# A statically ordered attention and MLP kernel: the order made anew with the sync queue's own issue times, large fetches in pieces, loads in order of use, memsets later

## Chip, cores, metric

One core of one Trainium2 chip. Time is device microseconds of a whole execution. The kernel before takes 810.61 us (median of 3 runs, 808.94 to 811.46). The profile's span, from first to last instruction, is about 2 us shorter than the time of the same execution (807.7 against 809.51); all stage times below are within the span. A profile is one execution.

## The reference, cut to what matters

```python
x: (1, 2048, 640); wqkv: (640, 1920); H = 32 heads of 20; F = 1536
g = sigmoid((x * gate_w).sum(-1))
a = softmax_attention(x, wqkv, wo)                 # scores, softmax, values, output projection
h = x @ w1 + b1;  b = (h * tanh(softplus(h))) @ w2 # mish
out = g * a + (1 - g) * b
```

## The kernel before

A list scheduler in Python (`Order`) runs when the program is built. Every piece of work is a `Task` with an engine, a declared cost, dependencies, a priority and a place in the order (`after`). It keeps a clock for each engine and emits the pieces as their turn comes. What runs on the chip is the resulting fixed sequence on each engine, with semaphores between engines. A declared cost is therefore never executed; it only moves work about in the sequence.

The attention works on groups G of four heads by 512 queries. Of a group's 16 key tiles, `SHARE[G]` go through VectorE (an approximate exponential by integer arithmetic), the others through ScalarE's exponential, two instructions of 128 x 1024 each. The last group is cut in two halves.

```python
class Task:                      # (cut)
        self.need, self.issue = 1e9, 450      # ns for which the sync queue is believed taken by one issue
...
    ld_x = {0: [load_x(("AQ", "SP")[s % 2], s, s + 1, 4200) for s in range(4)]}   # AQ: ACT's DMA queue
    ld_w0 = [load(("SP", "AQ")[t], w0[:, t], ..., 4500) for t in range(2)]        # first queries', keys' weights
    ld_x[1] = [load_x("SP", 4, 8, 6500)]
    ld_wv = load("SP", wv, w_src[:, :, 2 * D:3 * D], 8000)                        # values' weights
    ld_x[2] = [load_x("AQ", 8, 12, 9000)]
...
    # each group's end: denominators gathered, inverted, spread to DRAM, broadcast, multiplied
    t1 = o.add("SP", 2200, gather, [t0], prio=0, key=G)
    t2 = o.add("DVE", 245, rec, [t1], prio=2, key=G)
    t3 = o.add("SP", 2200, spread, [t2], prio=0, key=G)      # "rows<-rec" in the profile: 8 KB, 4 KB for the half group at the end
    t4 = o.add("SP", 3000, bcast, [t3], prio=0, key=G, rings=[rb])   # "rbc<-rows", 4 DMAs
    t5 = o.add("DVE", 690, norm, [t4], ...)                  # "on<-oraw,rbc"
...
    # near the end: heads and MLP sums come back from DRAM, then the output projection
    def back(c):
        def fetch():
            if c < 3:
                nc.sync.dma_start(out=bs_of(c)..., in_=bsd[c])                       # 640 KB
            nc.sync.dma_start(out=ocs[c][:, 0:KT - 1, :], in_=ocd[c]...)             # 512 KB, "w<-oc"
            nc.sync.dma_start(out=ocs[c][0:48, KT - 1, :], in_=ocd[c][(KT - 1) * P:...])
```

The projection of the first two quarters of the output uses PSUM tile X, of which there is one; that of the last two uses the three S tiles. VectorE mixes the result with the MLP's ("xt<-X,g,w") and so frees the tile.

The softmax here doesn't subtract the row's maximum and nothing guards it: scores larger than these inputs give would overflow.

## Time and profile before

| stage (us of the span) | before |
|---|---|
| start to first exponential | 11.93 |
| first to 22nd exponential | 24.76 |
| 22nd to end of the last of 740 | 749.0 |
| tail, after the last exponential | 22.0 |
| ScalarE idle: up to the 22nd / from there to the last | 5.1 / 10.0 |

The 22nd exponential is a fair post for the end of the start, at about 36 us, when loads end. ScalarE and TensorE are each about 95% busy, so look at the two ends and at gaps. The prediction shows the lines.

### The profile page before, as it was taken

To read this page: it belongs to the slowest core of one execution; us is meant where nothing else is said; L and a number is where in the kernel's file an instruction comes from. 1 tells how busy PE (TensorE), PEld (TensorE's weight loads), DVE (VectorE), ACT (ScalarE), POOL (GpSimd) and SP (SyncE) were. 2 spreads that over 40 slices of the span, in tenths; PEclk is the share of its full clock that TensorE was granted. 3 is DMA by queue.
4 is the path that set the end of the run, shared out by engine and by line. 5 is a ranking of instruction groups with operands and counts; after the bars stand their busy time and mean duration, and the time that the engine had idled before them with its cause. 6 is when DMAs were issued, how large, how long until landed. Compare 5 with 4: busy or idle time off the path is not lost.

```text
span 807.7 us, 25538 instructions
## 1 busy us (share of the span) xinstructions
PE 768.4 (95%) x11228; PEld 279.7 (35%) x11228; DVE 683.4 (85%) x906; ACT 763.3 (95%) x791; POOL 9.7 (1%) x12
## 2 busy tenths in 40 slices
PE   7999999999899998999999999899999997999978
PEld 3433223222443334333323332433223222243445
DVE  3699799999977878999798789889999998978934
ACT  4899999999999999999999999999999999899990
POOL 4000000000000000000000000000000000000000
PEclk9999999999999999999999999999999999999999
DMA  9602100112001000011110112111100002212132
GB/s 309 199 23 57 27 23 23 36 46 65 21 29 46 23 24 25 20 54 35 48 30 22 26 35 68 30 37 38 28 10 20 19 19 81 72 28 72 37 87 84
DMA packets 45608, 39.88 MB, mean 49 GB/s; under 512 B 20244, under 2 KB 39380, under 8 KB 45496
## 3 DMA queue, kind: packets, MB, share of 16 engines
q1 hardware_dynamic: 44024, 37.14, 15.9%
q8 instruction: 88, 1.44, 0.8%
q10 hardware_dynamic: 1472, 1.10, 0.4%
q14 instruction: 24, 0.20, 0.1%
HBM read 26.63 MB, written 11.08 MB: 47 GB/s over the span
## 4 chain that ended last, share of the span: by engine, by line
PE 51%; ACT 33%; DVE 7%; DMA 5%; issue 3%; SPq 1%; DVEq 0%; ACTq 0%
ACT es L890 26%; PE S L865 20%; PE C L848 15%; PE X L584 10%; ACT arena L1071 6%; PE X L667 3%; DVE t L924 3%; PE S L584 2%; DMA rbc<-rows 1%; DMA rows<-rec 1%; DMA wvt<-in_A_wqkv_dram 1%; DVE t L938 1%; ACT L1070 1%; PE X L646 1%; SPq L1018 1%
## 5 line engine op out<-in xcount | busy, mean ns | idle before, releaser
L890 ACT ACTIVATE es<-S 128x1024 bf16<-128x1024 f32 x740 | 683.1, 1131 | 16.7 <-PE S L865 16.0
L924 DVE TENSOR_SCALAR t<-S 128x1024 uint16<-128x1024 f32 x284 | 345.5, 1219 | 34.9 <-PE S L865 33.6
L865 PE MATMUL S<-qs,kt 32*128 32x512 bf16 (+1 forms) x2112 | 313.0, 376 | 14.5 <-ACT es L890 6.7
L865 PEld LDWEIGHTS <-kt 32*128 32x128 bf16 x2112 | 94.4, 91 | 282.3 <-issue 271.1
L938 DVE TENSOR_SCALAR t<-t 128x2048 uint16<-128x2048 uint16 x284 | 186.7, 683 | 3.8 <-PE C L848 2.2
L848 PE MATMUL C<-es,va 128*32 128x512 bf16 (+1 forms) x1536 | 136.3, 379 | 0.5 <-DVE oraw L972 0.4
L848 PE MATMUL C<-t,vs 128*32 128x512 bf16 (+1 forms) x1152 | 103.1, 380 | 0.9 <-DVE t L938 0.6
L584 PE MATMUL X<-xt,w 128*32 128x512 bf16 x960 | 75.3, 383 | 1.2 <-DVE arena L1057 1.2
L584 PE MATMUL X<-w,arena 128*32 128x320 bf16 x1536 | 76.3, 305 | 0.1
L848 PEld LDWEIGHTS <-va 128*32 128x32 bf16 x2112 | 48.7, 95 | 73.7 <-issue 66.0
L1071 ACT ACTIVATE arena<-arena 128x2048 bf16<-128x2048 bf16 x36 | 69.1, 1939 | 0.3
L848 PE MATMUL C<-t,va 128*32 128x512 bf16 (+1 forms) x576 | 56.2, 379 | 2.8 <-DVE oraw L972 2.3
L584 PEld LDWEIGHTS <-arena 128*32 128x32 bf16 x1856 | 41.4, 96 | 41.3 <-issue 33.1
L667 PE MATMUL X<-xt,wqk 128*32 128x512 bf16 (+1 forms) x640 | 51.0, 383 | 0.0
L584 PEld LDWEIGHTS <-w 128*32 128x32 bf16 (+1 forms) x1280 | 29.0, 97 | 34.2 <-issue 27.1
L848 PEld LDWEIGHTS <-vs 128*32 128x32 bf16 x1152 | 29.5, 95 | 31.3 <-issue 25.9
L1057 DVE TENSOR_SCALAR arena<-X,b 128x512 bf16<-128x512 f32 x48 | 35.8, 745 | 4.7 <-PE X L584 4.6
L584 PE MATMUL X<-wvt,xt 128*32 128x160 bf16 x1240 | 28.2, 233 | 8.0 <-DVE va L724 4.8
L1025 DVE TENSOR_TENSOR on<-oraw,rbc 128x512 bf16<-128x512 f32 (+1 forms) x32 | 21.7, 678 | 13.8 <-DMA rbc<-rows 13.5
L584 PEld LDWEIGHTS <-xt 128*32 128x32 bf16 x1280 | 23.4, 96 | 18.1 <-issue 16.2
L673 DVE CAST g<-X 120x512 bf16<-120x512 f32 x32 | 21.9, 684 | 3.9 <-PE X L667 3.8
L972 DVE COPY oraw<-C 128x512 f32<-128x512 f32 (+1 forms) x33 | 22.0, 667 | 1.3 <-PE C L848 1.3
(80 smaller groups left out, 249.2 us busy)
## 6 DMA issues: line engine op xcount, KB each, us to landing
rbc<-rows SPq DMA_DIRECT2D x124, 64.0 KB
w<-in_B_w_dram SPq DMA_DIRECT2D x2, 1920.0 KB
out_dram<-xt SPq DMA_DIRECT2D x16, 160.0 KB
oc<-on SPq DMA_DIRECT2D x112, 20.0 KB
k<-g SPq DMA_DIRECT2D x16, 120.0 KB
kt<-k SPq DMA_DIRECT2D x24, 80.0 KB
q<-g SPq DMA_DIRECT2D x16, 120.0 KB
qs<-q SPq DMA_DIRECT2D x96, 20.0 KB
```

What stands on the lines that cost most here:

```text
L584: nc.tensor.matmul(t[32 * r:32 * r + 32, 0:width], lhsT=lhsT(r), rhs=rhs, start=a, stop=b, tile_position=(0, 32 * r))
L667: nc.tensor.matmul(t[32 * r:32 * r + w, 0:QC], lhsT=wqk[:, k, a:a + w], rhs=xt[:, c, k, :], start=k == 0, stop=k == KT - 1, tile_position= ...
L673: nc.vector.tensor_copy(out=gb.tile, in_=t[0:120, 0:QC])
L848: nc.tensor.matmul(acc[G][32 * r:32 * r + 32, qa:qb], lhsT=vs4[:, b, term - 1, DVE_KEYS.index(j), h:h + 32] if term else va4[:, b, j, h:h ...
L865: nc.tensor.matmul(t[:, (off + a) * QC + i * w:(off + a) * QC + (i + 1) * w], lhsT=kt[32 * r:32 * r + 32, (p % 2) * S + j * P:(p % 2) * S ...
L890: nc.scalar.activation(eb.tile[:, 0:w * QC], sb.tile[:, 0:w * QC], ACT.Exp, scale=inv)
L924: nc.vector.tensor_scalar(out=bufs[0].tile[:, 2 * QC * hp:2 * QC * (hp + 1)], in0=xb.tile, scalar1=P * LOG2E * inv, scalar2=P * (127 - log ...
L938: (nc.vector if eng == "DVE" else nc.gpsimd).tensor_scalar(out=bufs[i].tile[:, a * w:(a + 1) * w], in0=bufs[0].tile[:, a * w:(a + 1) * w], ...
L972: nc.vector.tensor_copy(out=ob.tile[:, a:b], in_=acc[G][:, a:b])
L1025: nc.vector.tensor_tensor(out=nb.tile[:, qa:qb], in0=ob.tile[:, qa:qb], in1=rb.tile[:, qa:qb], op=ALU.mult)
L1057: lambda t: nc.vector.tensor_scalar(out=hs[:, ft, :], in0=t[:, 0:QC], scalar1=b1[:, ft:ft + 1], scalar2=None, op0=ALU.add),
L1071: nc.scalar.activation(v, hs[:, 4 * a:4 * a + 4, :] if i == 0 else v, func, bias=1.0 if i == 1 else 0.0)
```

## The change

Intent: give the scheduler the sync queue's real issue times, so that its order fits the chip better; split fetches so that short transfers get between them; load x and then the values' weights on one queue in order of use; move memsets behind what is urgent; then choose the places of all work anew.

```diff
-SHARE = (2, 4, 4, 5, ... 5, 5, 2, 2)
+SHARE = (3, 6, 5, 2, ... 4, 3, 4, 4)
-DENSE = (0.8, 6.7, 11.35, 19.15)          # likewise MISH, DOWN, KEYS, QUERIES, VALUES
+DENSE = (1.25, 4.7, 11.7, 18.4)
-OUT = (26.25, 26.8, 28.9)
+OUT = (26.05, 27.7, 27.55)
-LEAD = 32
+LEAD = 24
-        self.need, self.issue = 1e9, 450
+        self.need, self.issue = 1e9, issue          # default 350
-    OVER = 900  LOW = 3  AHEAD = 8  EARLY = 600  BESIDE = 120
+    OVER = 1200 LOW = 2  AHEAD = 24 EARLY = 550  BESIDE = 30
-    nc.gpsimd.memset(kt[:, S:2 * S], 0.0)
-    nc.gpsimd.memset(qs, 0.0)
+    t_zero = [o.add("POOL", 1800, lambda a=a: nc.gpsimd.memset(a, 0.0), prio=3) for a in (kt[:, S:2 * S], qs)]
-    ld_x[1] = [load_x("SP", 4, 8, 6500)]
-    ld_wv = load("SP", wv, ..., 8000)
-    ld_x[2] = [load_x("AQ", 8, 12, 9000)]
-    ld_x[3] = [load_x("SP", 12, 16, 11000)]
+    ld_x[1] = [load_x("SP", 4, 8, 6000)]
+    ld_x[2] = [load_x("SP", 8, 12, 8000)]
+    ld_x[3] = [load_x("SP", 12, 16, 10000)]
+    ld_wv = load("SP", wv, ..., 12500)
-        for i in range(10):     # warm-up matmuls
+        for i in range(8):
-        t1 = o.add("SP", 2200, gather, ...)
+        t1 = o.add("SP", 2050, gather, ..., issue=560)
-        t3 = o.add("SP", 2200, spread, ...)
+        t3 = o.add("SP", 1600, spread, ..., issue=350)
-        t4 = o.add("SP", 3000, bcast, ...)
+        t4 = o.add("SP", 3600, bcast, ..., issue=1700)
-    def fetch(): (640 KB, 512 KB, 48 KB, one task)
+    t_back[c]: four tasks of 128 KB, one of 48 KB, four of 160 KB (issue=900 each)
... (issue times of other fetches, the late loads' place, cut)
```

More of the change, by code (lines that the diff above doesn't have):

```diff
@@ L34 @@
 DVE_KEYS = (1, 4, 7, 10, 13, 14)
-SHARE = (2, 4, 4, 5, 4, 5, 5, 6, 3, 3, 4, 5, 5, 6, 2, 5, 6, 3, 4, 6, 4, 4, 6, 6, 4, 5, 6, 6, 2, 5, 5, 2, 2)
-DENSE = (0.8, 6.7, 11.35, 19.15)
-MISH = (0.9, 3.35, 2.65, 4.9)
-DOWN = (-0.75, -1.85, 4.0, 8.2)
-KEYS = ((0, 0.95, 2.2), (1, 5.5, 5.65), (2, 11.55, 13.85), (3, 18.55, 19.15), (4, 24.1, 24.45))
-QUERIES = 1.6
-VALUES = ((1, 2.8), (2, 10.0), (3, 12.4))
-OUT = (26.25, 26.8, 28.9)
+SHARE = (3, 6, 5, 2, 5, 4, 4, 6, 3, 5, 5, 5, 5, 5, 4, 4, 6, 4, 3, 6, 5, 4, 5, 4, 5, 4, 6, 4, 5, 4, 3, 4, 4)
+DENSE = (1.25, 4.7, 11.7, 18.4)
+MISH = (2.4, 4.2, 0.25, 3.7)
+DOWN = (-0.85, -1.2, 4.15, 7.5)
+KEYS = ((0, 0.8, 1.45), (1, 5.2, 7.45), (2, 13.05, 14.0), (3, 17.65, 18.85), (4, 24.55, 25.05))
+QUERIES = 2.05
+VALUES = ((1, 3.1), (2, 10.6), (3, 12.7))
+OUT = (26.05, 27.7, 27.55)
 PAIRS = 8
@@ L97, in __init__ @@
     def __init__(self, eng, cost, fn, deps=(), after=None, prio=5, rings=(),
-                 frees=(), mode=None, rows=(), key=0, port=False, work=0):
+                 frees=(), mode=None, rows=(), key=0, port=False, work=0, issue=350):
         self.eng, self.cost, self.fn = eng, cost - (84 if eng == "DVE" else 0), fn
@@ L134 @@
     LAT = {"PE": 230, "ACT": 165, "DVE": 134}
-    OVER = 900
-    LOW = 3
-    AHEAD = 8
+    OVER = 1200
+    LOW = 2
+    AHEAD = 24
     LATE = 28
     HOLD = 650
-    EARLY = 600
-    BESIDE = 120
+    EARLY = 550
+    BESIDE = 30
     AHEAD_D = 2000
@@ L497 @@
     ld_w0 = [load(("SP", "AQ")[t], w0[:, t], w_src[:, :, D * t:D * t + 92], 4500) for t in range(2)]
-    ld_x[1] = [load_x("SP", 4, 8, 6500)]
-    ld_wv = load("SP", wv, w_src[:, :, 2 * D:3 * D], 8000)
-    ld_x[2] = [load_x("AQ", 8, 12, 9000)]
-    ld_x[3] = [load_x("SP", 12, 16, 11000)]
-    ld_wqk = load("SP", wqk[:, :, 0:2 * D], w_src[:, :, 0:2 * D], 14000)
-    ld_gw = load("SP", gw[:, :, 0:1], gate_w.rearrange("(kt p o) -> p kt o", p=P, o=1), 8000)
+    ld_x[1] = [load_x("SP", 4, 8, 6000)]
+    ld_x[2] = [load_x("SP", 8, 12, 8000)]
+    ld_x[3] = [load_x("SP", 12, 16, 10000)]
+    ld_wv = load("SP", wv, w_src[:, :, 2 * D:3 * D], 12500)
+    ld_wqk = load("SP", wqk[:, :, 0:2 * D], w_src[:, :, 0:2 * D], 17500)
+    ld_gw = load("SP", gw[:, :, 0:1], gate_w.rearrange("(kt p o) -> p kt o", p=P, o=1), 18500)
+    ld_wqk.issue, ld_gw.issue = 2600, 2400
     t_ident = o.add("POOL", 1500, lambda: make_identity(nc, ident), prio=0)
@@ L513 @@
     t_pad = o.add("POOL", 700, lambda: nc.gpsimd.memset(wov[:, 5, :], 0.0), prio=2)
-    t_va = o.add("POOL", 6000, lambda: nc.gpsimd.memset(va, 1.0), prio=1)
+    t_va = o.add("POOL", 5000, lambda: nc.gpsimd.memset(va, 1.0), prio=1)
+    t_zero = [o.add("POOL", 1800, lambda a=a: nc.gpsimd.memset(a, 0.0), prio=3) for a in (kt[:, S:2 * S], qs)]
     junk = Buf(R["X"])
@@ L520, in warm @@
         junk.tile = pt(junk)
-        for i in range(10):
+        for i in range(8):
             nc.tensor.matmul(junk.tile[:, :], lhsT=kt[:, 0:P], rhs=kt[:, 0:QC], start=True, stop=True)
-    t_warm = o.add("PE", 4300, warm, [], prio=1.05, mode="full", rings=[junk], frees=[junk])
+    t_warm = o.add("PE", 3900, warm, [], prio=1.05, mode="full", rings=[junk], frees=[junk])
     t_warm.key = -1
@@ L693, in fetch @@
                                   in_=kd[u][DH * i:DH * i + DH, :])
-        t = o.add("SP", 4600, fetch, [t_kd[u, c] for u in {u for _, u, _ in pieces(p)} for c in range(NQ)],
+        t = o.add("SP", 4600, fetch, t_zero + [t_kd[u, c] for u in {u for _, u, _ in pieces(p)} for c in range(NQ)],
                   prio=1, key=g_of(p, 0) - 1, rings=[k_buf[p]])
-        t.issue = 1800
+        t.issue = 1300
         for j in range(NS):
@@ L707, in fetch @@
                                   in_=qd[u][DH * i:DH * i + DH, c * QC:(c + 1) * QC])
-        t_q[G] = o.add("SP", 4000, fetch, [t_qd[u, c] for u in {u for _, u, _ in pieces(p)}],
+        t_q[G] = o.add("SP", 4000, fetch, t_zero + [t_qd[u, c] for u in {u for _, u, _ in pieces(p)}],
                        after=at(G - 1.7), prio=1, key=G - 0.5, rings=[q_buf[G]])
-        t_q[G].issue = 1800
+        t_q[G].issue = 1150
     def v_unit(b, js, after, key, prio=3, ring="X"):
@@ L802, in late_loads @@
             nc.sync.dma_start(out=wov[32 * r:32 * r + DH, 5, :], in_=A_wo[560 + DH * r:560 + DH * (r + 1)])
-    t_late = o.add("SP", 20000, late_loads, [ld_wqk, t_pad], after=at(0.15), prio=1)
+    t_late = o.add("SP", 20000, late_loads, [ld_wqk, t_pad], prio=1, issue=16000)
     t_b1 = o.add("DVE", 150, lambda: nc.vector.tensor_copy(out=b1, in_=b1b), [t_late], after=at(1.0), prio=3)
@@ L1002, in gather @@
             nc.sync.dma_start(out=den["d"][:, 0:n], in_=ob.tile[DH:P:32, qa:qb])
-        t1 = o.add("SP", 2200, gather, [t0], prio=0, key=G)
+        t1 = o.add("SP", 2050, gather, [t0], prio=0, key=G, issue=560)
         def rec(den=den, n=n):
@@ L1012, in spread @@
             nc.sync.dma_start(out=den["m"].rearrange("(a b) -> a b", b=n), in_=den["r"][:, 0:n])
-        t3 = o.add("SP", 2200, spread, [t2], prio=0, key=G)
+        t3 = o.add("SP", 1600, spread, [t2], prio=0, key=G, issue=350)
         def bcast(rb=rb, den=den, w=w, qa=qa, qb=qb):
@@ L1019, in bcast @@
                                   in_=den["m"][r * w:(r + 1) * w].partition_broadcast(32))
-        t4 = o.add("SP", 3000, bcast, [t3], prio=0, key=G, rings=[rb])
+        t4 = o.add("SP", 3600, bcast, [t3], prio=0, key=G, rings=[rb], issue=1700)
         def norm(G=G, ob=ob, rb=rb, nb=nb, qa=qa, qb=qb):
@@ L1041 @@
         last = [o.add("SP", 3000, place, [t5], prio=0, key=G, frees=[nb])]
-        last[-1].issue = 1800
+        last[-1].issue = 2900 if p == NP - 1 else 1400
         t_on[G] = (t0, last)
@@ L1116, in back, with heads, rest @@
     def back(c):
-        def fetch():
-            if c < 3:
-                nc.sync.dma_start(out=bs_of(c).rearrange("p u c -> p (u c)"), in_=bsd[c])
-            nc.sync.dma_start(out=ocs[c][:, 0:KT - 1, :],
-                              in_=ocd[c][0:(KT - 1) * P].rearrange("(k p) q -> p k q", p=P))
-            nc.sync.dma_start(out=ocs[c][0:48, KT - 1, :], in_=ocd[c][(KT - 1) * P:(KT - 1) * P + 48])
-        t_back[c] = o.add(
-            "SP", 7000, fetch, free_of[c] + [t for p in range(NP - 1) for t in t_on[g_of(p, c)][1]]
-            + ([t_bd[c, u] for u in range(NU)] + [t_h[3, ft] for ft in range(FT)] if c < 3 else []), prio=1, key=24 + c)
-        t_back[c].issue = 1500
+        def heads(lo, hi):
+            nc.sync.dma_start(out=ocs[c][:, lo:hi, :], in_=ocd[c][lo * P:hi * P].rearrange("(k p) q -> p k q", p=P))
+        def rest():
+            nc.sync.dma_start(out=ocs[c][0:48, KT - 1, :], in_=ocd[c][(KT - 1) * P:(KT - 1) * P + 48])
+        deps = free_of[c] + [t for p in range(NP - 1) for t in t_on[g_of(p, c)][1]]
+        t_back[c] = [o.add("SP", 2900, f, deps, prio=1, key=24 + c, issue=900) for f in (
+            lambda: heads(0, 1), lambda: heads(1, 2), lambda: heads(2, 3), lambda: heads(3, 4), rest)]
+        if c < 3:
+            for u in range(NU):
+                t_back[c].append(o.add(
+                    "SP", 2900, lambda u=u: nc.sync.dma_start(out=bs_of(c)[:, u, :], in_=bsd[c][:, u * D:(u + 1) * D]),
+                    [t_bd[c, u]] + ([t_h[3, ft] for ft in range(FT)] if c < 2 else free_of[c]), prio=1, key=24 + c, issue=900))
     def f_mm(c, u, hf, k, t):
@@ L1150, in f_deps @@
     def f_deps(c, u):
-        return [t_back[c], t_q[NG - 1]] + [t_b[c, u, i] for i in range(2)]
+        return t_back[c] + [t_q[NG - 1]] + [t_b[c, u, i] for i in range(2)]
     def f_unit(c, u, hf, after, key):
```

## The prediction

> **What bounds the kernel now.** I read the page first (busy shares, slices, chain), then the busy time by stage, then ScalarE's waits, then the timeline of the first 36 us and of the last 40 us, and last the sync queue's issues.
>
> ```profile
> PE 768.4 (95%) x11228; PEld 279.7 (35%) x11228; DVE 683.4 (85%) x906; ACT 763.3 (95%) x791; POOL 9.7 (1%) x12
> ACT  4899999999999999999999999999999999899990
> PE 51%; ACT 33%; DVE 7%; DMA 5%; issue 3%; SPq 1%; DVEq 0%; ACTq 0%
> L890 ACT ACTIVATE es<-S 128x1024 bf16<-128x1024 f32 x740 | 683.1, 1131 | 16.7 <-PE S L865 16.0
> ```
>
> ScalarE (ACT) and TensorE are both at 95%, and the chain changes between them all the time. ScalarE's 740 exponentials are 683.1 us, 0.923 us each in sequence; the 1131 ns includes overlap of neighbours. TensorE's figure is softer: 23.6 us of its 768.4 are the filler matmuls of the helper that keeps it warm (22.8 + 0.8 in its groups). ScalarE is idle only at the two ends, so I cut the span there.
>
> ```profile
> 0.00:11.93 11.93, 9.12 (x102) 4.47 (x102) 3.48 (x15) 2.56 (x4) 9.17 (x10) 1.00 0.83 261
> 11.93:36.00 24.07, 20.77 (x404) 10.99 (x406) 12.71 (x25) 18.98 (x21) 0.00 (x0) 1.00 0.87 296
> 785.70:807.70 22.00, 17.24 (x410) 11.64 (x409) 9.73 (x14) 2.11 (x4) 0.00 (x0) 0.92 0.23 78
> ```
>
> The columns are the stretch and its length, then busy us of PE, weight load, DVE, ACT and POOL, clock, DMA share, GB/s. So: 11.93 us before the first exponential; 773.8 us from it to the end of the last one, of which ACT is busy 763.3 - 2.56 - 2.11 = 758.6 and idle 15.2; and 22.0 us of tail in which TensorE finishes the output projection. 11.9 + 773.8 + 22.0 = 807.7, and the timed median, 810.6, is 2.9 more. The DMA engines are 83 to 87% busy in the first 36 us, so there the order of loads matters.
>
> ```profile
> 11.93 1.94 ACT L890 ACTIVATE es<-S 128x1024 bf16<-128x1024 f32 x2 [2.11 <-PE S L865]
> 15.48 5.61 ACT L890 ACTIVATE es<-S 128x1024 bf16<-128x1024 f32 x6 [1.61 <-PE S L865]
> 22.18 5.61 ACT L890 ACTIVATE es<-S 128x1024 bf16<-128x1024 f32 x6 [1.09 <-PE S L865]
> 29.43 5.61 ACT L890 ACTIVATE es<-S 128x1024 bf16<-128x1024 f32 x6 [1.65 <-PE S L865]
> 13.89 0.88 PE L584 MATMUL X<-wvt,xt 128*32 128x160 bf16 x40 [1.85 <-DMA wvt<-in_A_wqkv_dram]
> ```
>
> Of the 15.2 us, 5.1 lie before 36 us (these three and 0.73 at 35.77). The last line is why: TensorE, which takes its queue in order, stands at the values' projection until its weights land, and the next scores are behind it. They had been issued at 3.78 and landed at 13.85. The remaining 10 us are a dozen gaps of 0.4 to 0.9 and one of 1.90 at 687.
>
> ```profile
> 775.59 1.01 SPq L1120 DMA_DIRECT2D w<-oc  x1
> 777.87 4.49 DMA rows<-rec
> 783.67 2.07 DMA rbc<-rows
> 785.86 0.42 DVE L1025 TENSOR_TENSOR on<-oraw,rbc 128x256 bf16<-128x256 f32 x1 [4.57 <-DMA rbc<-rows]
> 786.80 1.15 PE L584 MATMUL X<-wo,arena 128*32 128x320 bf16 x20 [3.38 <-DVE xt L1140]
> 788.13 2.79 PE L584 MATMUL S<-wo,w 128*32 128x320 bf16 x40
> 790.95 1.55 PE L584 MATMUL S<-wo,w 128*32 128x320 bf16 x40
> ```
>
> This is the tail. A 512 KB fetch of heads goes out at 775.59; the 8 KB row of reciprocals behind it takes 4.49 us, where the same step at 117.83 lets its successor go after 1.48. VectorE waits 4.57 us for it, TensorE 3.38 for VectorE, and then runs cold: 40 matmuls in 2.79 us against 1.55 a little later. After that TensorE works almost without a break to 804.05, so this wait is on the path to the end.
>
> **What the Trainium skill says.** "DMA: Bandwidth & Descriptors", section "Issuing engines are not separate DMA queues": DMAs of all issuing engines run on the same 16 engines and interleave, and issuing from several saves only sequencer time. The trace agrees: the keys' first weights (115 KB, issued on ACT's queue at 1.66 with 640 KB of x right behind them and 640 KB of x on SP's) let their matmuls go only at 9.65. Section "Queues, rings and completion order" of that page: each engine takes one ring's descriptors in order and round-robins between rings. So x on one queue should land chunk by chunk in order of use. "TensorE: Matmul & The Clock Gate", section "What's actually happening": half clock after an idle window of about 3.4 us. The 3.38 us wait and the 2.79 against 1.55 agree. "Perfetto Trace Analysis", section "DMA Instruction — HWDGE (DVE, Sync)": a DMA instruction's slice is descriptor generation, the data moves outside it. It agrees: the reciprocals' issue is 0.36 us, its landing 4.49.
>
> **The change, part by part.** The kernel's static instruction order is made by a list scheduler from declared costs; nearly all of the diff feeds it better costs or other places. The arithmetic stays the same.
>
> *Share.* The sum goes from 144 to 147. By the kernel's rules the full groups' sum stays 140 to 139, so ACT gets 2 exponentials more there, and the two half groups go from 2 to 4 each, which takes 2 of 14 from each. 740 becomes 738: 2 x 0.923 = **-1.8 us** of ACT. VectorE's batches go from 142 to 143, one more of 2 x 1.22 + 2 x 0.68 = 3.8 us, on an engine at 85%: nothing.
>
> *Start.* Two warm-up matmuls fewer are 2 x 0.427 = 0.85 us (the warm-up starts at 1.19 and the transposes at 5.42, at once after it). The zeroings of kt and qs (1.80 and 1.38 us) leave the front of GpSimd's queue, so the identity is ready about 3 us sooner than 4.36; without this the shorter warm-up would save little. ACT's queue carries no x behind the keys' weights, and the second chunk of x shares the engines with nothing but small weights. Before, scores first went at 11.49, behind transposes that waited for x until 10.94. I take query weights at 7.6 instead of 7.86, keys' matmuls straight after the queries' (8.9 instead of 9.65), keys copied out by 9.7, first exponential at 10.4: **-1.5 us** (my estimate from these rows).
>
> *Values' weights after x.* Before, the order believed them there 6 us after x's first pieces; they came 4 us later than that. Now x takes 2.62 MB, with the small weights 2.85, and they end 3.65 MB into the stream: at the 296 GB/s of the stage that is 12.3 us, plus the start and the landing delay, some 14 to 15.5. So they arrive no sooner, but the order now puts transposes, keys and scores of the next chunk ahead of them. I expect the 1.85 us wait gone and half of ACT's 5.1 us: **-2.5 us**. Not all, since TensorE is busy 20.77 of these 24.07 us.
>
> *Issue times.* The order believed 450 ns for nearly every issue; the trace has 0.34 (rows), 0.55 (den), 1.70 (four broadcasts), 1.39 (four places). The new figures are these. The sync queue is mostly waiting, so this only orders queues better. Middle gaps, 10 us: I give **-1**, with at least 3 either way, since a new order makes new gaps.
>
> *Pieces.* A 512 KB fetch becomes four of 128 KB, 640 KB become four of 160 KB, each its own task, so that reciprocals and broadcasts can slip in between. At 776 this could give back 3.38 us of wait and (2.79 - 1.55) + (1.15 - 0.86) = 1.5 us of cold clock, 4.9 in all. That the new order places them well is likely, not sure; OUT's later place for the second quarter also moves work toward the end. I take 60%: **-3 us**.
>
> Sum: -1.8 - 1.5 - 2.5 - 1 - 3 = -9.8, so 800.8. Scheduler gains are seldom kept in full on the chip; I take back 1.2 and predict **802 us**.
>
> **Rivals.** (1) *The order is not the limit*: TensorE at 95% simply fills every gap won, so only ACT's two exponentials and the shorter start count: about 807. For it: TensorE is busy 86% even in the stage with the wait. Against: 23.6 us of it is filler. (2) *A new wait*: the zeroing of qs now stands behind 4.9 + 0.63 + 1.80 us of GpSimd work, so it ends near 10 us, and if it is issued after the first query copy, the first scores wait for it (and would read zeros); or all of x on one queue delays the third chunk, which had a queue to itself; or pieces cost the sync queue issue time just before the end. 808 to 812. (3) *Everything fits*: tail 4.9, start 5, middle gaps halved, 1.8: about 794.
>
> **Range and chances.** The ends are the two stages I can size; the middle is the noise, 3 us each way. 802 with +7 for (1) and half of (2), -6 for most of (3): 796 to 809. Over 2% faster means under 794.4, all of (3): 0.06. Over 2% slower means 826.8, for which no part of the profile has a size: 0.02.
>
> **What would show it.** First exponential at 10.4 rather than 11.93; idle of ACT between it and 36 us near 2.5; no TensorE wait on wvt of over 0.5 us at 12 to 16 us; 738 exponentials; last exponential to end of span 19 us rather than 22.0, with no wait over 2 us on broadcasts and a clock near 1 in that stage. It is wrong if the first score waits for GpSimd, if ACT's middle idle is over 14 us, or if the tail keeps its 3.4 us wait.

## The result, and the profile after

800.49 us (median of 4 runs, 799.74 to 801.13) against 809.91 us for the kernel before beside it (4 runs); ratio 0.9882, interval 0.9861 to 0.9902. That is 1.2% faster and clear of noise. A ratio is the mean time of one kernel's fast runs over that of the other's fast runs of the same rounds, so not quite the ratio of the medians quoted. 802 had been predicted, 796 to 809 as the range.

From the page of the kernel after: busy time of the engines, and the exponentials' group.

```profile
PE 763.0 (96%) x11326; PEld 272.7 (34%) x11326; DVE 686.7 (86%) x910; ACT 760.6 (95%) x789; POOL 9.8 (1%) x12
L891 ACT ACTIVATE es<-S 128x1024 bf16<-128x1024 f32 x738 | 680.3, 1128 | 13.8 <-PE S L866 13.4
```

738 exponentials, as counted; nothing else in these sums tells where 9.8 us of span went. The stages of the kernel after, in the columns of the prediction's table, do:

```profile
0.00:11.27 11.27, 8.86 (x102) 5.28 (x103) 3.77 (x15) 2.56 (x4) 9.24 (x10) 1.00 0.83 263
11.27:36.63 25.36, 22.90 (x446) 11.43 (x445) 17.02 (x31) 19.83 (x22) 0.00 (x0) 1.00 0.84 287
779.66:797.90 18.24, 14.29 (x375) 9.15 (x366) 9.09 (x13) 2.08 (x4) 0.00 (x0) 1.00 0.33 112
```

| stage | before | after | difference | predicted |
|---|---|---|---|---|
| to the first exponential | 11.93 | 11.27 | -0.7 | -1.5 |
| first to 22nd | 24.76 | 25.26 | +0.5 | -2.5 |
| 22nd to the end of the last | 749.0 | 743.1 | -5.9 | -1.8 (two exponentials) - 1 |
| tail | 22.0 | 18.3 | -3.7 | -3 |
| span | 807.7 | 797.9 | -9.8 | -9.8 |

The sum is the predicted one to a tenth before the shading, and that is partly luck: the start gave nothing (-0.2 instead of -4), the middle four times what was put down for it. In the middle ScalarE's idle time fell from 10.0 to 6.9 us, its busy time by 2.7 us (1.8 for the two exponentials).

The start. ScalarE's exponentials in the timeline of the kernel after:

```profile
11.27 12.99 ACT L891 ACTIVATE es<-S 128x1024 bf16<-128x1024 f32 x14 [1.91 <-PE S L866]
27.20 2.15 ACT L891 ACTIVATE es<-S 128x1024 bf16<-128x1024 f32 x2 [2.94 <-PE S L866]
29.74 3.77 ACT L891 ACTIVATE es<-S 128x1024 bf16<-128x1024 f32 x4 [0.39 <-PE S L866]
35.61 22.30 ACT L891 ACTIVATE es<-S 128x1024 bf16<-128x1024 f32 x24 [2.10 <-PE S L866]
```

Fourteen in a row, without the wait on the values' weights, which no engine waits for now. Then the keys of the second chunk run out, and ScalarE stands 2.94 + 0.39 + 2.10 = 5.4 us where it stood 5.1. The first of these gaps begins on TensorE: between 15.4 and 22.5 us it finishes the second chunk's keys, makes the next group's queries and four pieces of values, and only at 22.64 transposes more of x for the keys of the next chunk. The last gap, 2.10 us, is VectorE's. The chain of work (`--critical`) runs through VectorE from 25.96 to 35.07 without a break: keys, three of its own exponentials, then the copy of x that later keys need, and at last those keys:

```profile
26.62 3.48 DVE L925 TENSOR_SCALAR t<-S 128x1024 uint16<-128x1024 f32 x3
30.02 0.68 DVE L558 COPY xt<-X 128x1024 bf16<-128x1024 bf16 x1
34.31 0.75 DVE L629 TENSOR_SCALAR kt<-S,mask 128x512 bf16<-128x512 f32 x1
```

The new shares give VectorE more exponentials in the first groups (3 and 6 key tiles instead of 2 and 4). By the 22nd of ScalarE's it has begun 16 of its own where it had begun 13, and it is busy 16.9 us of this stage instead of 12.7. The same chain stands in a_again and a_loads below. No run changes these shares alone, so the chain is all that shows it.

Why the first exponential came at 11.27 and not at 10.4, from the same timeline:

```profile
8.77 0.58 ACT L651 CAST qs<-S 128x512 bf16<-128x512 f32 x1 [2.19 <-PE S L647]
9.41 1.38 POOL L515 MEMSET qs<- 128x1536 bf16 x1 [0.95 <-ACT qs L651]
10.84 0.40 PE L866 MATMUL S<-qs,kt 32*128 32x512 bf16 x4 [0.47 <-POOL qs L515]
```

This is the wait that the prediction named as a rival. ScalarE writes the first queries into slot 0 of `qs` at 8.77; GpSimd then zeroes all three slots, slot 0 too, having waited for the copy; the first scores wait for GpSimd. It costs 0.47 us, but it is worse than that: the first four heads' first 512 queries are zero when the scores are made. All runs of the experiments were called correct all the same; the scores are so small that the softmax is nearly flat. Worked out on the host from the reference's inputs, not measured on the chip, zero queries there change the output by at most 1.3e-5 where its standard deviation is 1.3e-3. It is a fault of the change all the same, and one that a tolerance cannot see.

The tail, in the timeline of the kernel after, sync queue first:

```profile
773.60 0.32 SPq L1013 DMA_DIRECT2D rows<-rec  x1
773.97 0.92 SPq L1119 DMA_DIRECT2D w<-oc  x2
776.95 1.71 SPq L1019 DMA_DIRECT2D rbc<-rows  x4
779.22 0.72 PE L585 MATMUL S<-wo,w 128*32 128x320 bf16 x16
780.17 0.43 DVE L1026 TENSOR_TENSOR on<-oraw,rbc 128x256 bf16<-128x256 f32 x1 [2.00 <-DMA rbc<-rows]
782.08 5.73 PE L585 MATMUL S<-wo,w 128*32 128x320 bf16 x160
```

Pieces do stand on both sides of the reciprocals now, and their row takes 776.95 - 773.60 = 3.35 us to release the broadcast instead of 4.51. But the normalisation starts 0.51 us after the last exponential ends (779.66), where before it started 0.13 after it (785.86 against 785.73). In this execution it is not sooner. VectorE still waits 2.00 us; TensorE does not, because its next work is on the S tiles, while before it had yet another unit on the single X tile, which VectorE could not free.

### The profile page after: what moved, and what is told of

It reads as the page before. It is cut to its first block, busy times and chain, and to the rows that moved or that the text cites. A ratio compares the mean times of both kernels' runs of the same rounds, so it can differ in the third digit from the quotient of the medians.

```text
span 797.9 us, 25753 instructions
## 1 busy us (share of the span) xinstructions
PE 763.0 (96%) x11326; PEld 272.7 (34%) x11326; DVE 686.7 (86%) x910; ACT 760.6 (95%) x789; POOL 9.8 (1%) x12
## 4 chain that ended last, share of the span: by engine, by line
PE 49%; ACT 38%; DVE 7%; DMA 3%; issue 3%; SPq 1%; POOL 0%; DVEq 0%; ACTq 0%
ACT es L891 28%; PE S L866 18%; PE C L849 13%; PE X L585 10%; ACT arena L1072 8%; DVE t L925 3%; PE X L668 2%; PE S L585 2%; DVE t L939 1%; DMA rows<-rec 1%; DMA rbc<-rows 1%; PE X L625 1%; PE X L647 1%; ACT L1072 1%; ACT L1071 1%
## 5 line engine op out<-in xcount | busy, mean ns | idle before, releaser
L866 PE MATMUL S<-qs,kt 32*128 32x512 bf16 (+1 forms) x2112 | 302.6, 376 | 15.2 <-ACT es L891 11.3
L939 DVE TENSOR_SCALAR t<-t 128x2048 uint16<-128x2048 uint16 x286 | 189.3, 684 | 7.2 <-PE C L849 5.5
L866 PEld LDWEIGHTS <-kt 32*128 32x128 bf16 x2112 | 90.6, 91 | 288.3 <-issue 280.3
L585 PE MATMUL X<-w,arena 128*32 128x320 bf16 x1536 | 78.3, 302 | 0.2
L585 PEld LDWEIGHTS <-w 128*32 128x32 bf16 (+1 forms) x1280 | 27.2, 95 | 33.4 <-issue 27.8
L463 PE MATMUL C<-wqk,gw 128*32 128x512 bf16 (+4 forms) x380 | 26.3, 368 | 0.0
```

The costliest lines, as they stand in the source:

```text
L463: nc.tensor.matmul(t[32 * r:32 * r + 32, a:a + n], lhsT=gw[:, 0, 1:33], rhs=wqk[:, r, 0:n], start=G is None, stop=G is None, tile_position ...
L585: nc.tensor.matmul(t[32 * r:32 * r + 32, 0:width], lhsT=lhsT(r), rhs=rhs, start=a, stop=b, tile_position=(0, 32 * r))
L866: nc.tensor.matmul(t[:, (off + a) * QC + i * w:(off + a) * QC + (i + 1) * w], lhsT=kt[32 * r:32 * r + 32, (p % 2) * S + j * P:(p % 2) * S ...
L939: (nc.vector if eng == "DVE" else nc.gpsimd).tensor_scalar(out=bufs[i].tile[:, a * w:(a + 1) * w], in0=bufs[0].tile[:, a * w:(a + 1) * w], ...
```

## The experiments

Theories. *Order* (mine after the comparison): the tail's gain is the sequence on TensorE and VectorE; pieces, and the loads' queue, do little of themselves; the middle's gain is the new places with the costs that go with them. *Transfers* (the prediction's): pieces let the reciprocals through, and loads in order of use feed the start.

Many experiments keep the order of every engine as it was and change only what is issued at a place in it ("order kept"); that was checked by comparing the instruction sequences. The others make the order anew. In the table, "first exp." and "22nd" are the starts of these exponentials, "middle" goes from the 22nd to the end of the last, "tail" from there to the end of the span. The table has each run's timed ratio to the kernel before, with its interval, and the stages of its profiled execution. `a_` runs start from the kernel after, `b_` runs from the kernel before.

| run | us, median | ratio (95%) | first exp. | 22nd | middle | tail |
|---|---|---|---|---|---|---|
| before | 810.61 | 1 | 11.93 | 36.69 | 749.0 | 22.0 |
| after | 800.49 | 0.9882 (0.9861 to 0.9902) | 11.27 | 36.53 | 743.1 | 18.3 |
| b_swap | 807.99 | 0.9971 (0.9937 to 1.0005) | 11.85 | 40.44 | 748.5 | 17.0 |
| b_pieces | 812.47 | 1.0045 (1.0018 to 1.0072) | 11.58 | 35.84 | 751.0 | 22.4 |
| a_merge | 801.78 | 0.9915 (0.9887 to 0.9943) | 10.94 | 36.19 | 742.9 | 18.7 |
| a_zero | 797.40 | 0.9869 (0.9839 to 0.9899) | 10.36 | 35.68 | 741.4 | 17.7 |
| b_loads | 812.52 | 1.0025 (0.9986 to 1.0065) | 10.39 | 41.52 | 749.2 | 19.2 |
| a_loads | 800.20 | 0.9872 (0.9834 to 0.9911) | 11.35 | 37.18 | 740.8 | 17.8 |
| b_issue | 818.83 | 1.0110 (1.0062 to 1.0157) | 12.17 | 41.41 | 757.4 | 18.3 |
| b_tune | 806.91 | 0.9964 (0.9910 to 1.0017) | 11.28 | 41.73 | 742.7 | 20.3 |
| a_again | 799.36 | 0.9857 (0.9821 to 0.9892) | 10.55 | 35.80 | 741.8 | 17.8 |
| a_zero2 | 798.17 | 0.9845 (0.9807 to 0.9883) | 10.69 | 36.00 | 742.6 | 17.7 |
| a_oldissue | 809.27 | 0.9974 (0.9930 to 1.0018) | 11.40 | 36.66 | 750.2 | 18.8 |
| a_jit | 802.97 | 0.9906 (0.9871 to 0.9942) | 11.18 | 36.43 | 741.1 | 23.8 |

The first four ran on one chip, the next four and the last four in two later batches on two other chips, each batch with its own runs of the kernel before (medians 807.91, 809.70 and 810.03).

### b_swap: before, two VectorE instructions exchanged (order otherwise kept)

```diff
         t5 = o.add("DVE", 690, norm, [t4], ...)
+        t5.defer = G == NG - 2      # emitted behind VectorE's next instruction, a mix
```

> The kernel before with two VectorE instructions exchanged near its end and nothing else: the first half group's normalisation, which waits 4.57 us for the broadcast at 785.86, goes behind the projection's mix that stands next to it. Order theory (the tail's gain came from TensorE no longer standing behind that wait): TensorE's wait of 3.38 us and the cold clock go, the tail shrinks from 22.0 to 17.5 to 19 us, the time falls by 3 to 4.5 us (ratio 0.9945 to 0.9965). Pieces theory (only a faster passage of reciprocals and broadcasts can help): VectorE and TensorE wait elsewhere for the same broadcast, under 1 us is gained (ratio 0.999 to 1.001).

The tail went from 22.0 to 17.0 us. In its timeline, normalisation and mix, and what TensorE does meanwhile:

```profile
785.68 0.55 DVE L1148 SCALAR_TENSOR_TENSOR xt<-X,g,w 128x320 bf16<-128x320 f32 x1 [1.28 <-PE X L591]
786.60 0.86 PE L591 MATMUL X<-wo,arena 128*32 128x320 bf16 x20
787.51 1.53 PE L591 MATMUL S<-wo,w 128*32 128x320 bf16 x40
788.28 0.42 DVE L1032 TENSOR_TENSOR on<-oraw,rbc 128x256 bf16<-128x256 f32 x1 [2.04 <-DMA rbc<-rows]
```

The X tile is freed at 786.2, before the wait; TensorE goes on at full clock (40 matmuls in 1.53 us where it had been 2.79). The reciprocals' row is as slow as ever (3.75 us from its issue at 781.20 to the broadcast's at 784.95). So one exchanged pair takes the tail below that of the whole change, with transfers untouched. For the wait at the end the order theory holds: faster reciprocals are not needed to free TensorE.

But the timed gain is only 0.3%, not the expected 0.35 to 0.55%, and it is not clear of noise: six runs, four at 807.8 to 809.4 and two at 802.7 and 803.4. The profile, one of the four, shows where they lose: its 22nd exponential is at 40.44, 3.75 us later than in the kernel before, whose start has the very same order. The clock column (after POOL) of two stretches of the start, the kernel before first:

```profile
14.00:18.00 4.00, 3.75 (x101) 2.41 (x97) 1.74 (x5) 2.52 (x3) 0.00 (x0) 1.00 1.04 369
18.00:22.00 4.00, 3.98 (x89) 2.03 (x86) 2.08 (x4) 3.08 (x4) 0.00 (x0) 1.00 1.05 398
```

and b_swap:

```profile
14.00:18.00 4.00, 4.00 (x82) 2.03 (x72) 1.29 (x3) 2.05 (x2) 0.00 (x0) 0.56 1.06 372
18.00:22.00 4.00, 3.94 (x28) 1.64 (x25) 1.47 (x5) 2.96 (x3) 0.00 (x0) 0.50 1.03 401
```

TensorE's clock was at half from 14.5 to 24.7 us. It had just stood 1.86 us for the values' weights, as the kernel before does (1.85). The same wait, then, but TensorE was busy for only 1.31 us of the stretch from 10 to 14 us here, and for 2.14 us in the kernel before. So the wait has a second price that not every execution pays. Of the five profiles whose order puts TensorE behind the values' weights (before, b_swap, b_pieces, b_loads, b_tune), three show half clock somewhere between 13 and 25 us; of the eight with the start of the kernel after, none. (b_issue has another start, without that wait and without half clock.)

The mean granted clock of every execution agrees: 0.991 to 0.994 for the four slow ones, 0.997 and 1.000 for the two fast ones. These two, 802.67 and 803.35, stand against 806.68 and 807.51, the two executions of the kernel before with a clock of 0.998 on that chip. At like clock the exchange is thus worth some 4 us, which is what the order theory expected. It rests on two executions each.

### b_pieces: before, pieces at the old place (order kept)

```diff
-                nc.sync.dma_start(out=ocs[c][:, 0:KT - 1, :], in_=...)            # 512 KB
+                for k in range(KT - 1):
+                    nc.sync.dma_start(out=ocs[c][:, k:k + 1, :], in_=...)         # 4 x 128 KB; bs likewise
```

> The kernel before, every engine's order unchanged; only each large fetch near the end is issued as pieces (4 x 128 KB and 4 x 160 KB) one right after the other at the old place. Order theory: pieces of themselves do nothing, the 8 KB row behind them still takes 4 to 5 us, ratio 0.998 to 1.003. Pieces theory in its plain form (small transfers get in between pieces even on one queue): the row takes under 3 us and 2 to 3 us are gained, ratio 0.996 to 0.9975.

```profile
776.29 2.02 SPq L1122 DMA_DIRECT2D w<-oc  x4
779.35 0.38 SPq L1012 DMA_DIRECT2D rows<-rec  x1
782.66 1.71 SPq L1018 DMA_DIRECT2D rbc<-rows  x4
```

The row took 3.31 us here against 4.51, between the two expectations. But the pieces' own issues kept the sync queue, so that the row went out 0.99 us after the reciprocals were ready (0.02 in the kernel before): from there to the broadcast it is 4.30 us against 4.54. TensorE still stood 2.45 us for VectorE, and its clock was at half from 785.4 to 792.2 us (787.2 to 790.6 in the kernel before): tail 22.4. Timed, it is 0.45% slower, a little past what was expected. Its six executions have a mean clock of 0.990, those of the kernel before beside it 0.994, so more half clock goes with the loss; why there is more of it is not settled. Pieces alone gain nothing.

### a_merge: after, each quarter's four heads pieces as one (order kept)

```diff
         def heads(lo, hi):
+            if lo:
+                return
+            hi = KT - 1
             nc.sync.dma_start(out=ocs[c][:, lo:hi, :], in_=...)
```

> The kernel after, every engine's order unchanged; only the four heads pieces of 128 KB of a quarter are issued as one of 512 KB at the first piece's place. Pieces theory: the last quarter's fetch is again ahead of the reciprocals, their row takes 4.5 us instead of 3.35, and the tail goes from 18.2 back to 21 us or more: 2.5 to 4 us slower than the kernel after (ratio to before 0.9915 to 0.9935). Order theory: the normalisation comes about 1 us later, but TensorE has other work queued ahead, so under 1 us is lost (ratio 0.988 to 0.9895).

```profile
771.68 0.39 SPq L1122 DMA_DIRECT2D w<-oc  x1
772.63 0.33 SPq L1013 DMA_DIRECT2D rows<-rec  x1
776.79 1.71 SPq L1019 DMA_DIRECT2D rbc<-rows  x4
```

With 512 KB ahead of it the row takes 4.16 us. In the kernel after it took 3.35 in the first profile, and in other profiles with the same pieces and order there 2.76 (a_again), 1.40 (a_zero), 1.48 (a_zero2) and 1.42 (a_loads); in the last three VectorE waits for the broadcast at most 0.24 us. So in this order pieces do let the reciprocals through. The tail of the profile is 18.7 us against 18.3 and 17.7 to 17.8: they are worth 0.4 to 1.0 us there. But that execution was the fastest of six (799.62; the others 801.2 to 804.8), and the timed ratio, 0.9915, is what the transfer theory expected, 0.3 to 0.7% above the unmerged kernels, though its interval reaches down to theirs. So by time the pieces may be worth 3 us, of which the profile shows 1 at most; where the rest would be, no profile shows. The other five executions had a lower clock (0.991 to 0.997) than the profiled one (0.998), so some of it may be half clock. It stays open.

### a_zero and a_zero2: after, the zeroing leaves out the first queries' slot (order kept)

```diff
-... for a in (kt[:, S:2 * S], qs)]
+... for a in (kt[:, S:2 * S], qs[:, QC:])]
```

> The kernel after, every order unchanged; the zeroing of the query tile leaves out the first slot, which the first queries fill whole, so it neither clears them nor holds the first scores. If that wait (0.47 us at 10.84) is on the path that sets the end: first exponential at 10.8 instead of 11.27 and the whole 0.4 to 0.5 us faster (ratio 0.9875 instead of 0.9882). If TensorE's work sets the pace of the first 36 us: first exponential 0.4 us earlier, but the 21st exponential starts where it did, within 0.2 us, and the time is the same. Either way the first head group's queries are right again, so the error against the reference should be equal or smaller.

> The kernel a_zero again, beside the kernel after on the same chip. If leaving the first slot out of the zeroing moves the whole start by what it moved the first exponential in its first profile (0.9 us at first and at the 22nd exponential, part of it the earlier landing in that execution): 0.5 to 1 us faster than a_again. If that was chance: the same as a_again within 0.3 us.

No wait on GpSimd is left. In the first profile the first exponential is 0.9 us earlier than after's and the 22nd 0.85, more than the 0.47 us of the wait. Beside the unchanged kernel on one chip (a_again, first exponential 10.55, 22nd 35.80) nothing of that is left in the profiles (10.69 and 36.00), and the medians, 798.17 and 799.36, differ by less than the runs scatter. So the wait's removal is not shown to gain time; the earlier starts of 10.4 to 10.7 us are the scatter of landings. The version is to be kept for its correct queries, at no cost.

### b_loads and a_loads: the loads exchanged (order of all computing engines kept)

```diff
 b_loads: sync queue  x1 x3 wq x[4:8] wv x[12:16]       ->  x1 x3 wq x[4:8] x[8:12] x[12:16] wv
          ACT's queue x0 x2 wk x[8:12]                  ->  x0 x2 wk
 a_loads: the reverse
```

> The kernel before, orders of all computing engines unchanged; only the loads are issued as in the kernel after (x on one queue, then the values' weights). If the loads' order of itself is what helps the start: no wait on the values' weights longer than before and 1 to 2 us gained (ratio 0.9975 to 0.999). If the gain needs TensorE's new order (my theory): TensorE still stands at the values' projection and the weights land later than 13.9, so its wait grows from 1.85 to 3 us or more, the granted clock falls to half in the next window as it did in the profile of b_swap (14.5 to 24.7 us), and 3 to 6 us are lost (ratio 1.004 to 1.008).

> The kernel after, orders of all computing engines unchanged; only the loads are issued as in the kernel before (values' weights after the second chunk of x, third chunk on ACT's queue). My theory: TensorE uses the values' weights only at 19.4 us, so nothing waits for them either way; the second chunk of x and the keys' first weights come 1 to 2 us later, so the first exponential goes from 11.27 to 12 to 13 us, but the 22nd starts within 0.7 us of where it did (36.5), since TensorE's work sets that pace: ratio 0.988 to 0.9895. If the loads matter by themselves, the 22nd exponential is 1.5 us or more later and the ratio over 0.9895.

In the timeline of b_loads, TensorE at the values' projection, then ScalarE's third exponential:

```profile
15.37 1.52 PE L596 MATMUL X<-wvt,xt 128*32 128x160 bf16 x40 [4.78 <-DMA wvt<-in_A_wqkv_dram]
18.13 2.10 ACT L902 ACTIVATE es<-S 128x1024 bf16<-128x1024 f32 x2 [5.80 <-PE S L877]
```

The first exponential came 1.5 us earlier (10.39), the very gain predicted for the whole of the start, though the kernel after alone scatters from 10.55 to 11.27; but with the old order TensorE's wait grew to 4.78 us, the clock was at half from 14.1 to 24.3 us, and the 22nd exponential was at 41.52, 4.8 us late. The timed loss is 0.25% and not clear of noise; less than expected, since its tail was shorter (19.2). TensorE at that tail:

```profile
790.89 0.86 PE L596 MATMUL X<-wo,arena 128*32 128x320 bf16 x20 [2.49 <-DVE xt L1152]
791.78 1.55 PE L596 MATMUL S<-wo,w 128*32 128x320 bf16 x40
```

It stood 2.49 us for VectorE, as long as in b_pieces, but at full clock afterwards. The orders of the two tails are the same, 19.2 and 22.4 us long; so about 3 us of the longer one is half clock, which may or may not come with the wait. In a_loads nothing waited for the values' weights, the 22nd exponential was 0.65 us later than in the kernel after, and the time was the same (0.9872); the first exponential, expected at 12 to 13, came at 11.35. So of the two parts of "values' weights after x", the order of work counts, and the order of loads is good only together with it.

### b_issue, b_tune, a_oldissue: costs and places apart (order made anew)

```diff
 b_issue    = before + issue times and landings of the sync queue's work as in the change
 b_tune     = before + SHARE, DENSE ... OUT, LEAD, OVER, LOW, AHEAD, EARLY, BESIDE as in the change
 a_oldissue = after with the sync queue's costs of before (450, 1800; 2200/2200/3000)
```

> The kernel before with only the declared costs of the sync queue's work set to those of the change (issue times, and landing 2050/1600/3600 for 2200/2200/3000), the order made anew with the old places of all work. If truer costs by themselves make the better order, as the change's intent says: a middle shorter by 3 us or more, ratio under 0.996. If the old places were fitted to the old costs and a new order is only as good as the search for its places: as slow as before or slower, ratio 0.998 to 1.02.

> The kernel before with only the places and the scheduler's constants of the change (shares, places of the dense parts, lead and limits), old costs, loads, memsets and fetches. If the gain sits in the new places alone: ratio 0.988 to 0.994. If places and costs are only good together: 0.998 to 1.02, with new waits on the sync queue's transfers or a longer tail.

> The kernel after with the declared costs of the sync queue's work put back to the old ones (issue 450, 1800 for gathers and places, landing 2200/2200/3000), everything else of the change kept, order made anew. If the truer issue times carry the middle's gain, as the change's intent says: middle 746 us or more, ratio over 0.992. If the new places and the declared loads carry it (b_tune's middle was 742.7 with old costs): middle 740 to 745, 22nd exponential near 36.5 us, ratio 0.986 to 0.991.

The change's costs with the old places are the worst kernel of all: middle 757.4 us. (They include the 16 us declared for the late loads, which the change also moves.) New places with the old costs give the whole middle gain (742.7) but a bad start, 41.73: TensorE stands behind the values' weights again (1.61 us, then half clock from 13.1 to 16.5), and ScalarE stands 5.99 us at 35 while TensorE makes keys. That the old declared landing of these weights is behind both is likely, not shown. And new places with the new loads but the old issue costs lose the middle again, 750.2 us: here the a_oldissue expectation that favoured the places fell. So neither part owns the gain: b_tune has it with the old costs, a_oldissue lacks it with the new places. What is shown is that orders made anew differ by this much.

Part of a_oldissue's loss is clock. In the profiles with the order of the kernel after, the middle is 740.8 to 741.8 us where no stretch of half clock falls in it (a_loads, a_zero, a_again) and 742.6 to 743.1 where one of 3.4 us does (a_zero2, a_merge, after), some 1.3 us more. The middle of a_oldissue has 13.6 us of half clock, four times as much: by this measure about 5 of the 8.4 us that it is behind a_again (an estimate from these profiles).

One of a_oldissue's gaps can be read to its cause. VectorE, TensorE, ScalarE in its timeline:

```profile
378.33 1.73 SPq L1018 DMA_DIRECT2D rbc<-rows  x4
383.29 0.69 DVE L1025 TENSOR_TENSOR on<-oraw,rbc 128x512 bf16<-128x512 f32 x1 [2.14 <-DMA rbc<-rows]
385.17 0.39 PE L865 MATMUL S<-qs,kt 32*128 32x512 bf16 x2 [1.49 <-DVE t L924]
386.96 1.02 ACT L890 ACTIVATE es<-S 128x1024 bf16<-128x1024 f32 x1 [1.88 <-PE S L865]
```

The order believed the broadcasts there 3.0 us after their issue; they took 4.96. VectorE stood 2.14 us, which held an S tile, TensorE 1.49, ScalarE 1.88. From 385.7 to 392.5 TensorE ran at half clock, and four more gaps of 0.3 to 0.55 us follow. The declared 3.6 of the change is still short of 4.96, so this shows how a wrong landing turns into idle time, not that the new figure is right.

### a_again and a_jit: how far one order speaks for others

```diff
-    EARLY = 550
+    EARLY = 560        # a_jit; a_again is the kernel after
```

> The kernel after, unchanged, as the baseline of this batch: ratio to before 0.986 to 0.990; first exponential near 11, the 22nd near 36.5, middle near 743, tail near 18.3 us in its profile; no half clock between 10 and 36 us.

> The kernel after with one constant of the scheduler moved by 10 ns of 550, which means nothing for any engine but makes another order from the middle on. It shows how much of the change is one well chosen order: if orders made with these costs are all about as good, the time is within 1 us of a_again; if the order kept is a pick among many, it is 2 to 7 us slower, most of it in the tail (ratio 0.990 to 0.997).

Ten nanoseconds in one rule of choice left the middle as it was (741.1 against 741.8) and made the tail 6.0 us longer (23.8 against 17.8). The end of it, TensorE:

```profile
792.47 0.86 PE L585 MATMUL X<-wo,arena 128*32 128x320 bf16 x20 [0.77 <-DVE xt L1145]
793.99 0.86 PE L585 MATMUL X<-wo,arena 128*32 128x320 bf16 x20 [0.65 <-DVE xt L1145]
795.50 0.86 PE L585 MATMUL X<-wo,arena 128*32 128x320 bf16 x20 [0.65 <-DVE xt L1145]
797.02 0.86 PE L585 MATMUL X<-wo,arena 128*32 128x320 bf16 x20 [0.65 <-DVE xt L1145]
```

Units of the single X tile were left over for the end, where each waits for VectorE. A tail of 18 us is thus a pick of this one order, not what the change's parts give by themselves. It is timed slower than a_again, 802.97 against 799.36, as the pick reading expected, by 3.6 us. The two profiles differ by 6.0 because that of a_again is its fastest execution (797.12).

## Why the prediction was right, and where it was not

- **The sum** was right: -9.8 us of span predicted before the shading, -9.8 measured. Its terms were not all.
- **Share**: right for ScalarE: 738 exponentials, two times 0.92 us. Busy time of the group fell by 2.8 us, 1 us more than two make; not explained. Wrong for VectorE, whose extra work it put at nothing "on an engine at 85%", an average: at the start, where the first groups' larger shares fall, the chain runs through VectorE.
- **Start, -1.5**: mis-sized, -0.7 in this execution. The step "first exponential at 10.4" missed the wait for the zeroing, which the prediction had only as a rival (0.47 us); landings make up the rest, for the same kernel gave 10.55 in another execution.
- **Values' weights, -2.5**: the mechanism was right (TensorE's wait on the weights is gone, with its order as the cause: b_loads and a_loads), the consequence wrong. The step "half of ACT's 5.1 us" failed: the idle time became 5.4 us in other places. Nearest is rival (1), no gain although the wait is gone, but not for its reason: TensorE did not fill what it gained, it had time for 32 filler matmuls before the 22nd exponential (12 before the change), and the last gap is VectorE's. What the prediction did not see is the other worth of that wait: 3.75 us of half clock in some executions (b_swap).
- **Middle, -1**: mis-sized. It is -4.1 us beside the two exponentials and comes from the order made anew; b_tune has it with the old costs, a_oldissue lacks it with the new places. Which part of the order makes it is open. The term was rightly called the noise, and a_oldissue and b_issue show its width: 7.1 and 14.3 us longer than in the kernel after.
- **Pieces, -3**: the size was near (-3.7), the reason mostly not. The step "pieces let reciprocals slip in, so the wait and the cold clock go" holds in its first half and fails in the second: the row is 1.2 to 3.1 us faster, but the wait and the cold clock went because TensorE's next work no longer stood behind VectorE, which the sequence alone can do (b_swap, with a slow row), and the same pieces in the order of a_jit leave a tail of 23.8. In the profiled tail pieces are worth 0.4 to 1.0 us (a_merge). The cold clock was put at 1.5 us; beside b_loads it is 1.9 in the kernel before (2.8 us of tail, of which 0.9 is the later end of the wait) and 3.2 in b_pieces. The row at this place is 4 KB, not 8: it is that of half a group, while the 1.48 us at 117.83 are those of a whole one.
- **Its own signs**: the 738 exponentials, no wait on the values' weights, the tail (18.3 us at full clock, for 19) came true. The first exponential and ScalarE's idle time at the start (5.4 us for 2.5) did not, and one sign of being wrong did: the first score waits for GpSimd.

Open: why b_pieces has more half clock, why a_merge is slower by time than its profile explains, and which places make the middle.

## What to carry to other kernels

A wait near the end can often be taken off the path by exchanging two instructions of an in-order engine, so look at who stands behind it before making the awaited transfer faster. In a kernel ordered by a scheduler, truer costs alone may make the order worse (b_issue); judge a part of the change by an experiment that keeps the order. Compare executions of like granted clock before a difference of a few us is explained. And when a memset is moved later, look at what has been written by then; a flat softmax hides the fault.

## What the Trainium skill lacked or had wrong

- "TensorE: Matmul & The Clock Gate", section "What's actually happening", puts the return to half clock after an idle window of about 3.4 us. Here a wait of 1.86 us (b_swap; TensorE busy 1.31 of 4 us around it) was followed by half clock for 10.2 us, and one of 1.85 us in the kernel before (busy 2.14 of 4) by none; what share of a window must be busy is missing, and busy time alone does not decide it: in the kernel after the clock fell at 282.8 us behind 3.41 us of which TensorE was busy for 2.75.
- "DMA: Bandwidth & Descriptors", section "Issuing engines are not separate DMA queues": nothing lacking, as far as it was tested. With the third chunk of x on ACT's queue instead of the sync queue, and the values' weights ahead of it, the time was the same (a_loads, 0.9872 against 0.9857 to 0.9882).
- No page gives the time of a small transfer behind a large one on one queue: from the issue of a row of reciprocals to the issue that waits for it, it took 1.48 us with nothing ahead (8 KB), and for the 4 KB near the end 1.40 to 3.35 between pieces of 128 KB in one and the same order, 3.31 behind four of them in a row, and 3.71 (b_loads) to 4.51 (before) behind one of 512 KB.
